# First batch of a windowed attention: values on 64 rows, probabilities copied unscattered, another order of steps

## The chip, the core and the metric

The kernel runs on one core of one Trainium2 chip. A core has a matrix engine (TensorE, PE in the profile; its weight loads are listed apart as PEld), a vector engine (VectorE, DVE), a scalar engine (ScalarE, ACT), a general engine (GpSimd, POOL) and a queue that issues DMA transfers (SyncE, SP). The engines run side by side, each in its own order, and wait for one another through semaphores. PE reads SBUF and writes PSUM, an accumulation memory of eight banks of 512 float32 columns on 128 partitions; DVE and ACT read PSUM, POOL does not in this kernel. The metric is the device time of one execution in microseconds (us), the lower the better.

## The reference

Attention with a causal window over 8 batches, 8 heads, 576 positions and 64 columns, then a feed-forward layer over the 4608 tokens:

```python
rel = pos[:, None] - pos[None, :]
mask_plain = (rel >= 0) & (rel < window)
mask_dil = (rel >= 0) & (rel < window * dilation) & (rel % dilation == 0)
masks = np.stack([mask_plain if h < H // 2 else mask_dil for h in range(H)], axis=0)
scores = np.where(masks[None, :, :, :], scores, -1000000000.0)
scores = scores - np.max(scores, axis=-1, keepdims=True)
attn = np.exp(scores)
attn = attn / (np.sum(attn, axis=-1, keepdims=True) + 1e-09)
return np.matmul(attn, v).astype(np.float32)
...
h = x @ w_in
g = np.where(h > 0.0, h, alpha * (np.exp(np.minimum(h, 0.0)) - 1.0))
return (g @ w_out).astype(np.float32)
```

The window is 32 positions, the dilation 4, so every query sees at most 32 keys. For the heads with dilation the kernel orders positions by residue, so that their window is one of 32 neighbours too. The weights are 512 x 2048 and 2048 x 512, and arrive as 64-bit words that the kernel turns into float32.

## The kernel before

**Tiling of the attention.** Heads are taken in pairs (`hp` 0 to 3), one head on rows 0 to 63 and one on rows 64 to 127. The 576 queries of a pair are 6 units (`NU`) of 96 (`QB`), each of 3 blocks (`GU`) of 32 (`G`). A block of 32 queries sees 64 keys: its own 32 and the 32 before.

**The first batch** is written out by hand in `first_attention` (line 338), a generator for each pair, and the main loop (line 951) names the steps in order. A letter and a pair's number is a step:
- S: scores, 36 small matmuls on top of a mask that two matmuls lay into PSUM (each float32 matmul has two records in the trace).
- M: DVE takes the maxima and subtracts them (lines 356, 359), ACT takes the exponential (361). Here a load of weights is issued too, held by a small POOL copy (119) behind the maxima.
- P: DVE sums (363), adds 1e-9 (326), takes reciprocals (327); the multiply (328) is DVE's for pairs 0 and 3 and POOL's for pairs 1 and 2.
- T: PE transposes the probabilities, 12 matmuls against an identity, and the first head's four copies follow; U: the second head's four. These copies (381 on DVE, 383 on ACT) scatter the 64 keys x 96 queries of a unit into a tile `pt` of 128 keys x 96 queries, where each block of 32 queries has its own 64 rows and the rest was set to zero.
- O: 12 matmuls of values (128 keys x 64) against those tiles, 96 columns each, and the copies to `x32`, the layer's input (314, 317).
- G: one term of the first product of the feed-forward layer (f = 0) for one pair; A, B, C, D: parts of the conversion of the first weights (A on ACT, line 136; B to D on DVE, lines 144, 152, 154).

All of these are marked so that each engine keeps them in program order. PSUM is shared by name: scores go to `a` or `b`, transposes to `c` or `a`, outputs to `d` or `b`, so an odd pair's transposes need `a` free and its outputs `b`.

**What follows.** The layer runs over chunks of 512 tokens; f counts the 16 slices of 128 hidden columns. Only pair 0 to 3 of the first batch feed the first chunk. Meanwhile DVE and ACT convert and split the weights (`magnitude`, `convert`, `split_w`) and do the second batch's attention (`second_attention`), whose order a planner sets from modelled times. The second batch's loads reuse the buffers `qt`, `kt` and `vt` of the first; weights go through rings `r0` to `r3`, of which `r2` and `r3` hold pairs 2 and 3 of the first batch until their outputs are made.

**Loads.** SP issues, in order, the masks, q and k of the four pairs, v of pairs 0 and 1, the first weights, v of pairs 2 and 3 (line 937).

Of the kernel before, what the change touches and what calls it, by code (L numbers as in the profile page):

```python
# [10 lines left out]
F32 = mybir.dt.float32  # L11
# [5 lines left out]
ALU = mybir.AluOpType  # L17

B, H, S, D = 8, 8, 576, 64
WINDOW, DIL = 32, 4  # L20
NCLS = S // DIL
DM, DFF = H * D, 2048
NT = B * S
P = 128
G = 32
QB = 3 * G
NU = S // QB
NPAIR = H // 2
NA = 3
GU = QB // G  # L30
# [30 lines left out]
WHEN = {1: (0, 6, 7, 13), 2: (0, 6, 7, 12)}  # L61
EARLY = 14
LAST = 14
OPER = 12
PLAIN = ("a5", "a-1'")
BLOCKS = [(b, hp) for b in range(CS + 1, B) for hp in (0, 2)]
# [5 lines left out]


@with_exitstack
def body(ctx: ExitStack, tc: tile.TileContext, q, k, v, masks, w_in, w_out, out):
    nc = tc.nc
    const = ctx.enter_context(tc.tile_pool(name="const", bufs=1))
    wst = ctx.enter_context(tc.tile_pool(name="wst", bufs=1))
    ap = ctx.enter_context(tc.tile_pool(name="ap", bufs=2))
    xp = ctx.enter_context(tc.tile_pool(name="xp", bufs=1))  # L80
# [8 lines left out]
    mask_sb = masks_sb[:, :2 * NU * 2 * G].rearrange("p (d m) -> p d m", d=2)  # L89
    ones_sb = masks_sb[:, 2 * NU * 2 * G:]  # L90
    ident = const.tile([QB, QB], F32, name="ident")

    pt = [const.tile([P, 2 * NU, QB], F32, name=f"pt{i}") for i in range(2)]

    early2 = [wst.tile([P, 2, 4 * DM], F32, name=f"r{NR - NE + i}") for i in range(NE)]
    early = [early2[i // 2][:, i % 2, :] for i in range(2 * NE)]
# [9 lines left out]
    def inorder(ins):  # L106
        tc.keep_in_program_order(ins)
        return ins
# [145 lines left out]
    last_transpose = [None] * B  # L254
    count = [0]

    def room(b, hp):
        i = b * NPAIR + hp
        if i in (2, 3):
            e = early[2 * (i - 2):]  # L260
            return e[0][:, :S], e[0][:, S:WINDOW + 2 * S], e[1][:, :2 * NU * D].rearrange("p (u d) -> p u d", u=2 * NU)
        return ap.tile([P, S], F32, name="qt"), ap.tile([P, WINDOW + S], F32, name="kt"), ap.tile([P, 2 * NU, D], F32, name="vt")


    qk_of, v_of = {}, {}
# [55 lines left out]
    def outputs(b, hp, places, vt, tr, keep=lambda ins: ins):  # L321
        products(places, vt, tr)
        return copies(b, hp, places, keep)

    def normalise(eng, sm, sums, keep):
        keep(nc.vector.tensor_scalar(out=sums, in0=sums, scalar1=1e-9, scalar2=None, op0=ALU.add))
        keep(nc.vector.reciprocal(out=sums, in_=sums))
        return keep(eng.tensor_tensor(out=sm, in0=sm, in1=sums.unsqueeze(2).broadcast_to([QB, 2 * NU, 2 * G]), op=ALU.mult))

    def transposed():  # L330
        count[0] += 1
        return pt[count[0] % len(pt)]
# [5 lines left out]
    def first_attention(hp, loaded):  # L338

        dil = hp >= NPAIR // 2  # L340
        qt, kt, vt = loaded
        if hp > 0:
            room, o = (early[0], WINDOW + 2 * S) if hp == 1 else (early[2 * (hp - 2) + 1], 2 * NU * D)
            sm = room[:QB, o:o + 2 * NU * 2 * G].rearrange("p (u j) -> p u j", u=2 * NU)
        else:
            sm = ap.tile([QB, 2 * NU, 2 * G], F32, name="sm", bufs=1)
        mx = ap.tile([QB, 2 * NU], F32, name="nmx", bufs=4)
        sums = ap.tile([QB, 2 * NU], F32, name="sums", bufs=4)
        s_ps = ps_f.tile([P, 2, TC], F32, name="ab"[hp % 2])[:QB, :, :NU * 2 * G]
        for h in range(2):  # L350
            mm(s_ps[:, h, :], ones_sb, mask_sb[:, int(dil), :], start=True, stop=False)
        scores([s_ps[:, h, :] for h in range(2)], qt, kt, False)
        yield
        s4 = s_ps.rearrange("p h (n j) -> p h n j", n=NU)
        mx4 = mx.rearrange("p (h n) -> p h n", h=2)
        inorder(nc.vector.tensor_reduce(out=mx4, in_=s4, op=ALU.max, axis=mybir.AxisListType.X))
        if hp > 0:
            load_w(hp, mx)
        inorder(nc.vector.tensor_tensor(out=sm.rearrange("p (h n) j -> p h n j", h=2), in0=s4,
                                        in1=mx4.unsqueeze(3).broadcast_to([QB, 2, NU, 2 * G]), op=ALU.subtract))  # L360
        inorder(nc.scalar.activation(out=sm, in_=sm, func=AF.Exp, scale=0.125))
        yield
        inorder(nc.vector.tensor_reduce(out=sums, in_=sm, op=ALU.add, axis=mybir.AxisListType.X))
        last = normalise(nc.vector if hp in (0, NPAIR - 1) else nc.gpsimd, sm, sums, inorder)
        if hp == NPAIR - 1:
            last_step[hp] = last.ins
        yield
        tr = transposed()

        t_ps = (ps_c, ps_f)[hp % 2].tile([P, 2, TC], F32, name="ca"[hp % 2])  # L370
        for n in range(NU):
            for h in range(2):
                o = n % NA * QB
                mm(t_ps[h * 2 * G:(h + 1) * 2 * G, n // NA, o:o + QB], sm[:, h * NU + n, :], ident, start=True, stop=True)
        t4 = t_ps[:, :, :NA * QB].rearrange("p i (n q) -> p i n q", n=NA)
        for h in range(2):
            to = tr[:, h * NU:(h + 1) * NU, :].rearrange("p (i n) q -> p i n q", i=2)
            for c, r, m in ((0, 0, 2), (1, 0, 1), (1, 1, 1), (2, 0, 2)):
                cs, ks, rs = slice(c * G, (c + 1) * G), slice((c + r) * G, (c + r + m) * G), slice((h * 2 + r) * G, (h * 2 + r + m) * G)
                if hp == NPAIR - 1 or (hp, h) == (1, 0):  # L380
                    inorder(nc.vector.tensor_copy(out=to[ks, :, :, cs], in_=t4[rs, :, :, cs]))
                else:
                    inorder(nc.scalar.copy(out=to[ks, :, :, cs], in_=t4[rs, :, :, cs]))  # L383
            yield
        a_ps = ps_f.tile([P, 2, TC], F32, name="db"[hp % 2])
        yield outputs(0, hp, [(a_ps[:, i, :], i * NA, (i + 1) * NA) for i in range(NU // NA)], vt, tr, inorder)

    def exponential(u, sm, nmx, sums):
        nc.scalar.activation(out=sm[:, u, :], in_=sm[:, u, :], func=AF.Exp, bias=nmx[:, u:u + 1], scale=0.125, accum_out=sums[:, u:u + 1])
# [542 lines left out]
                    load_v(i + 2)  # L932
            yield state[-1]

    rooms = [room(0, hp) for hp in range(NPAIR)]

    for what in "m0 qk0 qk1 qk2 qk3 v0 v1 w0 v2 v3".split():
        i = int(what[-1])
        if what[0] == "m":
            nc.sync.dma_start(out=masks_sb, in_=masks)  # L940
            nc.gpsimd.tensor_tensor(out=ident, in0=ones_sb, in1=ones_sb, op=ALU.mult)
        if what[0] == "w":
            load_w(i)
        for t, src in zip("qkv", (q, k, v)):
            if t in what:
                nc.sync.dma_start(out=rooms[i]["qkv".index(t)], in_=src[i])
    x32[0] = xp.tile([P, NPAIR, S], F32, name="x32", bufs=2)
    its = [first_attention(hp, rooms[hp]) for hp in range(NPAIR)]


    for what in "S0 S1 M0 M1 S2 P0 M2 T0 U0 S3 P1 P2 A0 M3 T1 U1 O0 T2 U2 P3 B0 O1 T3 U3 O2 G0 G1 O3 G2 A1 C0 D1".split():
        i = int(what[1])
        if what == "G0":
            ps_second.close()
            ps_h = ctx.enter_context(tc.tile_pool(name="ps_h", bufs=1, space=bass.MemoryType.PSUM, side="right"))
            first = product1(0, 0)
        if what[0] == "A":
            inorder(magnitude(i))
        elif what[0] in "BCD":
            last_conversion = convert(i // 2, inorder, {"B": slice(0, DM), "C": slice(DM, 2 * DM), "D": slice(2 * DM, 4 * DM)}[what[0]])  # L960
        elif what[0] == "G":
            next(first)
        else:
            last_copy = next(its[i])
# [117 lines left out]
def _layout(q, k, v):  # L1082


    order = np.arange(S).reshape(NCLS, DIL).T.reshape(-1)

    inner = np.arange(G).reshape(G // DIL, DIL).T.reshape(-1)
    plain = (np.arange(0, S, G)[:, None] + inner[None, :]).reshape(-1)
    qs = np.empty((B, NPAIR, 2 * D, S), np.float32)
    ks = np.zeros((B, NPAIR, 2 * D, WINDOW + S), np.float32)  # L1090
    vs = np.empty((B, NPAIR, P, 2, NU, D), np.float32)
    for hp in range(NPAIR):
        dil = hp >= NPAIR // 2
        hs = slice(2 * hp, 2 * hp + 2)
        qo, ko = (order, order) if dil else (plain, np.arange(S))
        qs[:, hp] = q[:, hs][:, :, qo].transpose(0, 1, 3, 2).reshape(B, 2 * D, S)
        ks[:, hp, :, WINDOW:] = k[:, hs][:, :, ko].transpose(0, 1, 3, 2).reshape(B, 2 * D, S)
        vv = np.zeros((B, 2, WINDOW + S, D), np.float32)
        vv[:, :, WINDOW:] = v[:, hs][:, :, ko]
        for n in range(NU):  # L1100
            vs[:, hp, :, :, n] = vv[:, :, n * QB:n * QB + P].transpose(0, 2, 1, 3)
    pairs = B * NPAIR
    return qs.reshape(pairs, P, S), ks.reshape(pairs, P, WINDOW + S), vs.reshape(pairs, P, 2 * NU, D), order


def _masks():
# [32 lines left out]
```

## Time and profile before

| | |
|---|---|
| median of 3 runs | 878.44 us (877.64 to 880.87) |
| profiled execution | 878.75 us |
| its span | 877.0 us |
| mean granted clock of PE | 0.995 |
| busy: PE, PEld, DVE, ACT, POOL | 97%, 82%, 63%, 62%, 4% of the span |
| chain that ended last, PE's part | 85% of the span |

The span runs from the first to the last instruction; a row of the profile names line, engine, operation, output and inputs, shapes, and how many instructions it holds, and a bracket at its end the idle time ahead of it and who ended that. Matmuls are pipelined, so that neighbouring rows of PE may overlap a little.

### The profile page before, as it was taken

The numbers are of one execution on the slowest core, as the hardware profiler recorded it, in microseconds if no ns is written. First come the engines' busy times: TensorE is split into PE (matmuls) and PEld (weight loads), VectorE is DVE, ScalarE is ACT, GpSimd is POOL, SyncE is SP. The second block draws the span as 40 slices with busy tenths as digits, with TensorE's granted clock in tenths as the row PEclk, the third lists the DMA queues.
The fourth block names the chain that finished last, engine by engine and source line by source line (L and its number), as shares of the span: only waits on it lengthen the run. The fifth ranks groups of instructions, "written<-read, shape, count | busy, mean of one in ns | idle before, by whom it ended". The sixth has DMA issues, their size and how long they took to land.

```text
span 877.0 us, 17535 instructions
## 1 busy us (share of the span) xinstructions
PE 854.6 (97%) x6788; PEld 721.9 (82%) x6788; DVE 553.5 (63%) x906; ACT 544.7 (62%) x1067; POOL 34.9 (4%) x72
## 2 busy tenths in 40 slices
PE   6999989999999999999999999999999999999998
PEld 4556777778878888898878899988898988999986
DVE  6899977657585866788665476645476645344431
ACT  3778977867576766666664565654466754555541
POOL 2000000000000000110010010100011100000000
PEclk8999999999999999999999999999999999999999
DMA  9997435032555256877753877762875652776541
GB/s 346 384 363 265 140 105 188 31 122 90 169 188 186 99 166 190 271 226 246 223 199 86 264 224 234 204 200 72 252 238 177 207 163 86 230 211 195 144 149 58
DMA packets 93459, 166.48 MB, mean 190 GB/s; under 512 B 9696, under 2 KB 40768, under 8 KB 93376
## 3 DMA queue, kind: packets, MB, share of 16 engines
q1 hardware_dynamic: 89200, 158.01, 56.8%
q10 hardware_dynamic: 4176, 7.34, 2.3%
q8 instruction: 54, 0.88, 0.4%
q14 instruction: 29, 0.24, 0.1%
HBM read 124.42 MB, written 40.89 MB: 189 GB/s over the span
## 4 chain that ended last, share of the span: by engine, by line
PE 85%; DVE 5%; ACT 5%; issue 2%; DMA 1%; SPq 0%; POOL 0%; ACTq 0%; DVEq 0%
PE o_ps L111 42%; PE h L111 35%; PE a_ps L111 8%; ACT pt L435 1%; DMA kt<-k 1%; DMA out<-e 1%; DVE nmx L410 1%; DVE sm L397 0%; ACT pt L383 0%; ACT h L624 0%; ACT gh L642 0%; DVE a L152 0%; ACT a L191 0%; ACT a L448 0%; ACT e L636 0%
## 5 line engine op out<-in xcount | busy, mean ns | idle before, releaser
L111 PE MATMUL h<-xall,r 128*128 128x384 f32 (+1 forms) x708 | 157.0, 363 | 1.2 <-ACT h L624 0.8
L111 PEld LDWEIGHTS h<-xall,r 128*128 128x128 f32 x708 | 127.4, 188 | 18.7 <-ACT h L624 1.2
L111 PE MATMUL o_ps<-a,gh 128*128 128x512 f32 x394 | 128.9, 416 | 0.0
L448 DVE SCALAR_TENSOR_TENSOR a-1_3369<-a-1_3369,a 128x768 f32<-128x768 f32 x64 | 61.0, 953 | 87.8 <-ACT a L448 87.8
L111 PE MATMUL h<-r,r 128*128 128x384 f32 x476 | 108.2, 336 | 1.0 <-DVE gl L448 0.9
L448 ACT COPY e<-h 128x384 f32<-128x384 f32 x96 | 46.0, 479 | 98.3 <-PE h L111 96.4
L448 ACT ACTIVATE a<-a-1_3369 128x384 f32<-128x384 f32 (+1 forms) x96 | 60.9, 634 | 50.1 <-DVE a-1_3369 L448 44.1
L111 PEld LDWEIGHTS o_ps<-a,gh 128*128 128x128 f32 x394 | 73.4, 188 | 21.8 <-issue 9.1
L111 PEld LDWEIGHTS h<-r,r 128*128 128x128 f32 x476 | 84.4, 188 | 4.3 <-DVE r L448 1.2
L111 PE MATMUL o_ps<-r,gh 128*128 128x512 f32 x242 | 75.3, 392 | 0.0
L111 PE MATMUL o_ps<-a,r 128*128 128x512 f32 x288 | 72.2, 392 | 0.0
L111 PE MATMUL o_ps<-a,gl 128*128 128x512 f32 x173 | 67.7, 391 | 0.0
L448 ACT ACTIVATE a<-a 128x768 f32<-128x768 f32 (+1 forms) x72 | 60.8, 845 | 1.9
L111 PEld LDWEIGHTS o_ps<-a,r 128*128 128x128 f32 x288 | 53.6, 188 | 9.9
L111 PE MATMUL h<-a,r 128*128 128x384 f32 x256 | 60.1, 335 | 0.0
L448 DVE TENSOR_TENSOR a-1_3369<-h,e 128x384 f32<-128x384 f32 x64 | 35.1, 549 | 35.5 <-PE h L111 35.5
L111 PEld LDWEIGHTS o_ps<-r,gh 128*128 128x128 f32 x242 | 44.9, 188 | 8.6
L111 PEld LDWEIGHTS h<-a,r 128*128 128x128 f32 x256 | 46.4, 188 | 4.2
L111 PE MATMUL o_ps<-r,gl 128*128 128x512 f32 x117 | 45.9, 392 | 0.2 <-DVE gl L448 0.2
L637 DVE SCALAR_TENSOR_TENSOR e<-h,e 128x512 f32<-128x512 f32 x30 | 20.6, 686 | 30.1 <-ACT e L636 29.9
L111 PE MATMUL o_ps<-a,xall 128*128 128x512 f32 x153 | 39.5, 393 | 0.0
L111 PEld LDWEIGHTS o_ps<-a,gl 128*128 128x128 f32 x173 | 32.5, 188 | 6.8
(217 smaller groups left out, 1531.3 us busy)
## 6 DMA issues: line engine op xcount, KB each, us to landing
r<-combined SPq DMA_DIRECT2D x224, 256.0 KB, 3.5
aside<-a-1_3369 SPq DMA_DIRECT2D x64, 192.0 KB, 3.3
vt<-v SPq DMA_DIRECT2D x30, 384.0 KB, 4.2
kt<-k SPq DMA_DIRECT2D x30, 304.0 KB, 4.7
qt<-q SPq DMA_DIRECT2D x30, 288.0 KB, 4.0
r<-w_in SPq DMA_DIRECT2D x16, 512.0 KB, 7.8
r<-w_out SPq DMA_DIRECT2D x16, 512.0 KB, 8.2
combined<-a SPq DMA_DIRECT2D x20, 256.0 KB, 3.0
```

The source lines that it names most:

```text
L111: return inorder(nc.tensor.matmul(*args, **kw))
L410: nc.vector.tensor_reduce(out=nmx, in_=sm, op=ALU.max, axis=mybir.AxisListType.X)
L435: last_transpose[b] = nc.scalar.copy(out=tr[ks, :, cs], in_=sm[cs, :, rs]).ins
L448: return lambda *args, **kw: inorder(getattr(self.eng, name)(*args, **kw))
L637: v.scalar_tensor_tensor(out=e, in0=h_ps, scalar=0.0, in1=e, op0=ALU.max, op1=ALU.subtract)
```

## The change

- **Values.** For the first batch the host lays out the values once more (`v0`): for each of 18 blocks of 32 queries its own 64 keys x 64 columns, one head of a pair on rows 0 to 63, the other on rows 64 to 127. A pair's load is 128 x 1152 float32 in place of 128 x 768. Pairs 0 and 1 keep it in one buffer of `x32` (which has two), pairs 2 and 3 where they had it.
- **Copies.** The transposed probabilities are copied as they stand in PSUM, two copies of 128 x 288 on ACT for a pair (step K), into a third of `turned`, a tile that takes the place of weights needed later. Nothing is scattered.
- **Outputs.** O becomes 36 matmuls for a pair, of 64 keys x 64 columns against 32 columns of `turned`; the copies to `x32` are a step of their own (X).
- **Normalising.** 1e-9 is added from a tile `least`; pair 0's multiply goes to POOL, so that only pair 3's stays on DVE.
- **Order.** The steps stand in another order (`SEQ`); S3 is ahead of the first transposes, and outputs, copies and transposes of different pairs alternate.

```diff
+SEQ = "S0 S1 M0 M1 S2 P0 M2 S3 T0 K0 P1 M3 O0 X0 T1 A0 K1 P2 O1 X1 P3 B0 T2 K2 T3 O2 K3 X2 G0 O3 A1 G1 G2 X3 C0 D1"
...
+    least = const.tile([QB, 2 * NU], F32, name="least")
+    nc.gpsimd.memset(least, 1e-9)
...
-    def room(b, hp):
-        i = b * NPAIR + hp
-        if i in (2, 3):
-            e = early[2 * (i - 2):]
-            return e[0][:, :S], e[0][:, S:WINDOW + 2 * S], e[1][:, :2 * NU * D].rearrange("p (u d) -> p u d", u=2 * NU)
-        return ap.tile([P, S], F32, name="qt"), ap.tile([P, WINDOW + S], F32, name="kt"), ap.tile([P, 2 * NU, D], F32, name="vt")
+    shared = xp.tile([P, 2, NU * GU * D], F32, name="x32", bufs=2)
+
+    def room(hp):
+        if hp > 1:
+            e = early[2 * (hp - 2):]
+            return e[0][:, :S], e[0][:, S:WINDOW + 2 * S], e[1][:, :NU * GU * D]
+        return ap.tile([P, S], F32, name="qt"), ap.tile([P, WINDOW + S], F32, name="kt"), shared[:, hp, :]
...
-    def normalise(eng, sm, sums, keep):
-        keep(nc.vector.tensor_scalar(out=sums, in0=sums, scalar1=1e-9, scalar2=None, op0=ALU.add))
+    def normalise(eng, sm, sums, keep, least=None):
+        if least is None:
+            keep(nc.vector.tensor_scalar(out=sums, in0=sums, scalar1=1e-9, scalar2=None, op0=ALU.add))
+        else:
+            keep(nc.vector.tensor_tensor(out=sums, in0=sums, in1=least, op=ALU.add))
...
-        last = normalise(nc.vector if hp in (0, NPAIR - 1) else nc.gpsimd, sm, sums, inorder)
+        last = normalise(nc.vector if hp == NPAIR - 1 else nc.gpsimd, sm, sums, inorder, least)
...
-        t4 = t_ps[:, :, :NA * QB].rearrange("p i (n q) -> p i n q", n=NA)
-        for h in range(2):
-            to = tr[:, h * NU:(h + 1) * NU, :].rearrange("p (i n) q -> p i n q", i=2)
-            for c, r, m in ((0, 0, 2), (1, 0, 1), (1, 1, 1), (2, 0, 2)):
-                cs, ks, rs = slice(c * G, (c + 1) * G), slice((c + r) * G, (c + r + m) * G), slice((h * 2 + r) * G, (h * 2 + r + m) * G)
-                if hp == NPAIR - 1 or (hp, h) == (1, 0):
-                    inorder(nc.vector.tensor_copy(out=to[ks, :, :, cs], in_=t4[rs, :, :, cs]))
-                else:
-                    inorder(nc.scalar.copy(out=to[ks, :, :, cs], in_=t4[rs, :, :, cs]))
-            yield
+        yield
+
+        tr = turned[:, hp % 3 * S:(hp % 3 + 1) * S]
+        for i in range(NU // NA):
+            inorder(nc.scalar.copy(out=tr[:, i * NA * QB:(i + 1) * NA * QB], in_=t_ps[:, i, :NA * QB]))
+        yield
         a_ps = ps_f.tile([P, 2, TC], F32, name="db"[hp % 2])
-        yield outputs(0, hp, [(a_ps[:, i, :], i * NA, (i + 1) * NA) for i in range(NU // NA)], vt, tr, inorder)
+        vt = vt.rearrange("p (n c d) -> p n c d", n=NU, c=GU)
+        for n in range(NU):
+            for c in range(GU):
+                for h in range(2):
+                    hs, o = slice(h * D, (h + 1) * D), n % NA * QB + c * G
+                    mm(a_ps[hs, n // NA, o:o + G], vt[hs, n, c, :], tr[hs, n * QB + c * G:n * QB + (c + 1) * G], start=True, stop=True)
+        yield
+        yield copies(0, hp, [(a_ps[:, i, :], i * NA, (i + 1) * NA) for i in range(NU // NA)], inorder)
...
-        for t, src in zip("qkv", (q, k, v)):
+        for t, src in zip("qkv", (q, k, v0)):
...
+    turned = wst.tile([P, 4, DM], F32, name="a5").rearrange("p t c -> p (t c)")
...
-    for what in "S0 S1 M0 M1 S2 P0 M2 T0 U0 S3 P1 P2 A0 M3 T1 U1 O0 T2 U2 P3 B0 O1 T3 U3 O2 G0 G1 O3 G2 A1 C0 D1".split():
+    for what in SEQ.split():
```

More of the change, by code (lines that the diff above doesn't have):

```diff
@@ L74, in body @@
 @with_exitstack
-def body(ctx: ExitStack, tc: tile.TileContext, q, k, v, masks, w_in, w_out, out):
+def body(ctx: ExitStack, tc: tile.TileContext, q, k, v, v0, masks, w_in, w_out, out):
     nc = tc.nc
@@ L342, in first_attention @@
         if hp > 0:
-            room, o = (early[0], WINDOW + 2 * S) if hp == 1 else (early[2 * (hp - 2) + 1], 2 * NU * D)
+            room, o = (early[0], WINDOW + 2 * S) if hp == 1 else (early[2 * (hp - 2) + 1], NU * GU * D)
             sm = room[:QB, o:o + 2 * NU * 2 * G].rearrange("p (u j) -> p u j", u=2 * NU)
@@ L367, in first_attention @@
         yield
-        tr = transposed()
         t_ps = (ps_c, ps_f)[hp % 2].tile([P, 2, TC], F32, name="ca"[hp % 2])
@@ L933, in second_attention @@
             yield state[-1]
-    rooms = [room(0, hp) for hp in range(NPAIR)]
+    rooms = [room(hp) for hp in range(NPAIR)]
     for what in "m0 qk0 qk1 qk2 qk3 v0 v1 w0 v2 v3".split():
@@ L1101, in _layout @@
             vs[:, hp, :, :, n] = vv[:, :, n * QB:n * QB + P].transpose(0, 2, 1, 3)
+    at = np.arange(NU)[:, None] * QB + np.arange(GU) * G + np.arange(2 * G)[:, None, None]
+    first = np.empty((NPAIR, 2, 2 * G, NU, GU, D), np.float32)
+    for hp in range(NPAIR):
+        vv = np.zeros((2, WINDOW + S, D), np.float32)
+        vv[:, WINDOW:] = v[0, 2 * hp:2 * hp + 2][:, order if hp >= NPAIR // 2 else np.arange(S)]
+        first[hp] = vv[:, at]
     pairs = B * NPAIR
-    return qs.reshape(pairs, P, S), ks.reshape(pairs, P, WINDOW + S), vs.reshape(pairs, P, 2 * NU, D), order
+    return qs.reshape(pairs, P, S), ks.reshape(pairs, P, WINDOW + S), vs.reshape(pairs, P, 2 * NU, D), first.reshape(NPAIR, P, NU * GU * D), order
 def _masks():
@@ L1124 @@
     from concourse.bass_utils import run_bass_kernel_spmd
-    qs, ks, vs, order = _layout(q, k, v)
+    qs, ks, vs, first, order = _layout(q, k, v)
     w_in = moe_w_in.reshape(NC, P, NF, P).transpose(2, 1, 0, 3).reshape(NF, P, DM)
-    arrays = {"q": qs, "k": ks, "v": vs, "masks": _masks(), "w_in": np.ascontiguousarray(w_in).view(np.int64),
+    arrays = {"q": qs, "k": ks, "v": vs, "v0": first, "masks": _masks(), "w_in": np.ascontiguousarray(w_in).view(np.int64),
               "w_out": np.ascontiguousarray(moe_w_out.reshape(NF, P, DM)).view(np.int64)}
```

## The prediction, made before the result was known

> **What bounds the kernel now.** I read the busy shares first, then busy times by stretch, TensorE's waits, and the engines' instructions in order of time. These are the busy shares; the busy times of two stretches (in order PE, PEld, DVE, ACT, POOL, clock, DMA share, GB/s); and the waits of PE.
>
> ```profile
> PE 854.6 (97%) x6788; PEld 721.9 (82%) x6788; DVE 553.5 (63%) x906; ACT 544.7 (62%) x1067; POOL 34.9 (4%) x72
> ...
> 0.00:28.20 28.20, 18.94 (x464) 15.14 (x464) 19.66 (x34) 13.20 (x30) 6.02 (x12) 0.88 0.95 358
> 28.20:48.00 19.80, 18.75 (x139) 9.18 (x138) 17.66 (x28) 12.81 (x21) 0.00 (x0) 1.00 1.01 382
> ...
> PE o_ps L111 <- DVE gl L643: 2.6, 1, 2.6
> ...
> PE h L111 <- DVE h L193: 1.0, 1, 1.0
> ...
> PE h L111 <- DVE e L634: 0.3, 1, 0.3
> ```
>
> PE is busy for 97% of the span, so a gain can only come from the little time in which it waits. 9.3 of that lie in the first 28.2 us (28.20 less 18.94), which is the stage that the change rewrites. Three later waits are for DVE: 1.0, 0.3 and 2.6, together 3.9 us, all ahead of products of the first chunk (L193 makes its weights, L634 and L643 its activations). The rows that set the order of the first stage, PE first:
>
> ```profile
> 10.17 1.52 PE L111 MATMUL a<-r 64*32 64x64 f32 x72
> 13.94 1.21 PE L111 MATMUL c<-ident,sm 96*64 96x96 f32 x24 [2.25 <-DVE sm L328]
> 15.08 0.87 PE L111 MATMUL b<-masks_sb 96*96 96x384 bf16 x2
> ...
> 18.61 2.19 PE L111 MATMUL a<-ident,r 96*64 96x96 f32 x24 [1.21 <-POOL r L328]
> 22.24 1.16 PE L111 MATMUL c<-ident,r 96*64 96x96 f32 x24
> ...
> 28.23 1.98 PE L111 MATMUL h<-x,a 128*128 128x512 f32 x4
> 30.15 1.21 PE L111 MATMUL b<-pt,r 128*64 128x96 f32 x24
> 31.29 5.43 PE L111 MATMUL h<-x,a 128*128 128x512 f32 x12
> 36.65 0.97 PE L111 MATMUL a_ps<-kt,qt 64*32 64x64 f32 x72
> ...
> 12.35 0.17 DVE L326 TENSOR_SCALAR sums<-sums 96x12 f32<-96x12 f32 x1
> 12.55 0.22 DVE L327 RECIPROCAL sums<-sums 96x12 f32<-96x12 f32 x1
> 12.81 0.95 DVE L328 TENSOR_TENSOR sm<-sm,sums 96x768 f32<-96x768 f32 x1
> 13.68 0.95 DVE L356 TENSOR_REDUCE nmx<-a 96x12 f32<-96x768 f32 x1
> 14.66 0.95 DVE L359 TENSOR_TENSOR r<-a,nmx 96x768 f32<-96x768 f32 x1
> 15.54 0.94 DVE L363 TENSOR_REDUCE sums<-r 96x12 f32<-96x768 f32 x1
> ...
> 17.78 0.80 DVE L326 TENSOR_SCALAR sums<-sums 96x12 f32<-96x12 f32 x1
> ...
> 20.92 1.44 DVE L381 COPY pt<-a 64x192 f32<-64x192 f32 x4 [0.28 <-PE a L111]
> ...
> 24.71 0.42 DVE L144 TENSOR_SCALAR a<-a 128x512 uint32<-128x512 uint32 x1
> ...
> 26.50 2.99 DVE L381 COPY pt<-a 64x192 f32<-64x192 f32 x8
> 33.18 0.69 DVE L144 TENSOR_SCALAR a<-a 128x1024 uint32<-128x1024 uint32 x1 [1.77 <-ACT a L136]
> ...
> 15.65 0.84 ACT L361 ACTIVATE r<-r 96x768 f32<-96x768 f32 x1 [3.33 <-DVE r L359]
> 16.40 2.64 ACT L383 COPY pt<-c 64x192 f32<-64x192 f32 x8
> 19.06 1.14 ACT L136 ACTIVATE a<-r 128x1024 f32<-128x1024 f32 x1
> 23.80 0.70 ACT L317 COPY x<-d 128x288 f32<-128x288 f32 x2
> ...
> 17.09 1.47 POOL L328 TENSOR_TENSOR r<-r,sums 96x768 f32<-96x768 f32 x1 [2.22 <-ACT pt L383]
> ```
>
> The last row of products, at 31.29, holds 12 records of the first gemm: four that end f = 0, eight that are f = 1. At 5.36/12 = 0.447 us each, f = 0 ends at 33.1: my mark for PE. My mark for DVE is 33.18, the conversion D1, which waits for ACT's A1, which stands behind the last copy of the attention. From D1 DVE works almost without a gap until PE's 1.0 us wait, so DVE sets the end as much as PE.
>
> **What the change does, step by step.** Scattering goes: eight copies a pair (2.64 on ACT; 1.44 and 2.99 on DVE) become two of 128x288, 0.70 a pair as in the row of L317. One multiply moves from DVE (0.95) to POOL (1.47). The sum with 1e-9 took 0.17, but 0.80 beside POOL's multiply; its tensor form I put at 0.17, bounds 0.17 and 0.80. DVE sheds 1.44 + 2.99 + 0.95 + 0.63 = 6.0 us, ACT 2.64 x 2 + 1.32 (half as many copies for pair 1) less 4 x 0.70 = 3.8.
>
> The products change from 24 records of 96 columns (1.20 us) to 72 of 32 columns, weights of 64 columns on 64 rows. No row shows them. The scores, also 72 records on 64 rows, took 0.97, 13.5 ns each, with weights of half as many columns; a record of the transposes, weights of 64 columns over 96 rows, took 1.16/24 = 48 ns. So the bounds are 0.97 and 72 x 48 = 3.5. I take 1.8, 25 ns a record: the score's record doubled for twice the columns, which is also the transposes' record halved for two halves of rows.
>
> [...]
>
> Now the new order, from the first place where it differs. S3 follows S2 (11.7), so it is done by 14.1. On DVE an M takes 1.86 (13.68 to 15.54), a P without its multiply 1.4 (0.94 + 0.17 + 0.22 and gaps), a conversion like B0 1.8 (24.71 to 26.50). So it runs M2 at 12.8 (no multiply before it), P1 at 14.7, M3 at 16.1, P2 at 18.0, P3 at 19.3 to 21.7 with its multiply, B0 and C0 until 25.3. POOL gives the first multiply at 14.3, P1's at 17.6, P2's at 20.9.
> PE and ACT: T0 14.35 to 15.5, K0 to 16.25, O0 to 18.1 and T1 to 19.3. On ACT the exponential of M3 stands ahead of X0 (18.0 to 18.85), then X0 to 19.55, A0 to 20.65, K1 to 21.35: PE idles two us and O1 runs 21.35 to 23.15. This added wait holds T2 behind O1 although its data is there at 20.9.
>
> The clock belongs in this sum. Granted clock by stretches (busy PE, clock, DMA share, GB/s):
>
> ```profile
> 11.60:15.00 3.40, 1.15 (x30) 1.00 1.01 403
> 15.00:18.40 3.40, 2.40 (x78) 0.52 1.05 393
> 18.40:21.90 3.50, 3.29 (x42) 0.50 1.03 408
> ```
>
> After a stretch with 1.15 us of work the clock was half for two stretches, and T1 took 2.19; T2 at 22.24, at full clock again, 1.16. In the new order 11.6 to 15 is full of S3 and T0, but 18.4 to 21.9 holds only 0.9 of T1 and 0.55 of O1. I let the clock fall at 21.9 for one stretch: T2 takes 2.2, to 25.35. Bounds: nothing, or T3 and O2 slow too (2.0 more). Then K2 to 26.1, T3 to 26.55, O2 to 28.35, X2 to 29.1, G0 to 29.3, O3 to 31.1, G1 and G2 to 32.9, the fourth term to 33.8 (X3 is done by 31.85). f = 0 ends **0.7 later** than the mark. A1 runs 29.1 to 30.25, so D1 starts at 30.3, **2.9 earlier**: DVE, not PE, gains.
>
> DMA: the values grow by half.
>
> ```profile
> vt<-v SPq DMA_DIRECT2D x1, 384.0 KB, 6.9
> ...
> 4.98 1.49 SPq L946 DMA_DIRECT2D vt<-v  x2
> 14.50 0.33 SPq L122 DMA_DIRECT2D r<-w_in  x1
> 15.74 0.33 SPq L122 DMA_DIRECT2D r<-w_out  x1
> ...
> r<-w_in SPq DMA_DIRECT2D x1, 512.0 KB, 8.7
> ...
> r<-w_out SPq DMA_DIRECT2D x1, 512.0 KB, 8.8
> ```
>
> Two weight loads land at 23.2 and 24.5, so 512 KB pass in 1.3 us with the queues full (DMA share about 1). Four times 192 KB more are 1.9 us. The second batch's first two value loads no longer wait for a buffer, so SP may issue their 768 KB ahead of these weights: 1.9 more. A1's weights then land at 26.4 to 28.4, before 29.1: hidden by the attention. Values of pair 0 land at 11.9 + 0.5, O0 begins at 16.3: hidden. If the cover goes, D1 is late by what lands after 29.1.
>
> Sum: +0.7 for PE's path; -1.0, since DVE is 2.9 ahead when PE waits for L193; of the two later waits (2.9), DVE's remaining lead, 2.9 - 0.3 = 2.6, can take 2.6; I take 2.1, since part can be lost to instructions that wait for PE itself (bounds 0 and 2.6). Together **-2.4**: span 877.0 to 874.6. The profiled execution took 878.75, 1.75 more than its span, and lies 0.3 over the median of 878.44; from the median the forecast is **876.0 us**.
>
> **Rivals.** (1) *Products one after another*, 3.5 us each: the end lies on the slower side. O0 ends at 19.8, K1 at 22.4, O1 at 25.9, O2 at 31.8, O3 at 36.2, f = 0 at about 39.0, 5.9 late; all of the 3.9 us of waits vanish, so +2.0: 880.4, and 884.3 if they stay. It decides from about 2.9 us a product, where 3.9 are lost. For it: both heads write one PSUM bank in one stretch, where the scores keep a bank for each. Against: their rows and output partitions are disjoint.
> [...]
> (2) *Transfers take the lead*: weights for the next conversions land 1.9 to 3.9 later and DVE waits for ACT, which waits for them; DVE's lead is gone, and PE's 0.7 is lost and at most the 1.0 won: 878.1 to 879.1, middle 878.6. For it: DMA share 1.01 until 48. This is also the case that the shorter copies bring nothing.
> (3) *Everything cheap*: products at 0.97 and full clock. ACT's chain still holds O1 to 21.35; O2 ends at 25.7, f = 0 at 31.2, 1.9 early; D1 starts 3.5 early; with the waits PE could win 5.8, DVE 3.5 to 6.0 (what it sheds). Taken 4.9: 873.5.
>
> **Chances.** Forecast 0.46; (1) 0.14; (2) 0.15; (3) 0.25. The range 872.4 to 881.0 leaves out about 0.05 of (1) and 0.1 of (3). A measurement here tells 0.5%, 4.4 us, from no change: faster 0.25 (0.2 of (3), 0.05 of the forecast's tail), slower 0.06 (from (1) and a clock that stays low), within 0.69.
>
> **What would show it.** Products of 72 records at 1.8 us (0.97: rival 3; 3.5: rival 1). K of 0.7 a pair. PE idle about 2 us ahead of O1, and a clock of 0.5 after it. D1 near 30.3 and f = 0 ending near 33.8. The wait for L193 gone, the 2.6 us wait for L643 mostly gone. I am wrong if DVE waits for L136 with late loads, or if a scheduler's other order of later instructions moves more than these 4 us.

## The result: 1.3% slower

| | before | after |
|---|---|---|
| median, us | 879.65 (877.64 to 881.47) | 891.24 (890.27 to 891.48) |
| span of the profiled execution, us | 877.0 | 889.7 |
| mean granted clock of PE | 0.995 | 0.983 |
| f = 0 of the layer's first product ends at, us | 33.1 | 47.8 |

The ratio is 1.013 [1.0103, 1.0157], from four runs of each. All four runs of the changed kernel have a mean granted clock of 0.981 to 0.986. The busy shares of the changed kernel:

```profile
PE 868.3 (98%) x6980; PEld 735.2 (83%) x6980; DVE 548.4 (62%) x893; ACT 541.0 (61%) x1055; POOL 36.8 (4%) x74
```

Its two first stretches (start and end, length, then busy PE, PEld, DVE, ACT, POOL, clock, DMA share, GB/s):

```profile
0.00:28.20 28.20, 18.45 (x466) 15.35 (x468) 17.10 (x27) 7.67 (x12) 7.48 (x14) 0.78 0.96 369
28.20:48.00 19.80, 19.80 (x228) 15.38 (x226) 3.33 (x4) 6.77 (x14) 0.00 (x0) 0.54 0.65 238
```

Two of PE's waits (in total, times, longest):

```profile
PE b L115 <- DVE nmx L364: 3.5, 1, 3.5
...
PE o_ps L115 <- DVE gl L653: 2.8, 2, 1.5
```

DVE and ACT shed 5.1 and 3.7 us, about what was forecast (6.0 and 3.8), but PE is busy 13.7 us longer. The second stretch tells where: PE works all 19.80 us at a mean clock of 0.54, and DVE, which did 17.66 us of work there before, does 3.33. Busy PE is here slow PE. The same first stage instruction by instruction (start, duration, engine, line, product, records, wait ahead):

```profile
14.07 0.53 PE L115 MATMUL b<-masks_sb 96*96 96x384 bf16 x2 [3.46 <-DVE nmx L364]
...
15.42 2.06 PE L115 MATMUL c<-ident,sm 96*64 96x96 f32 x24
17.97 1.81 PE L115 MATMUL d<-a,x 64*64 64x32 f32 x29 [0.49 <-ACT a L386]
20.37 2.55 PE L115 MATMUL d<-a,x 64*64 64x32 f32 x43 [0.59 <-issue]
22.85 2.19 PE L115 MATMUL a<-ident,r 96*64 96x96 f32 x24
25.54 4.05 PE L115 MATMUL b<-a,x 64*64 64x32 f32 x72 [0.50 <-ACT a L386]
29.52 2.19 PE L115 MATMUL c<-ident,r 96*64 96x96 f32 x24
31.49 2.13 PE L115 MATMUL a<-ident,r 96*64 96x96 f32 x24
33.55 4.05 PE L115 MATMUL d<-a,r 64*64 64x32 f32 x72
37.54 2.07 PE L115 MATMUL h<-x,a 128*128 128x512 f32 x2
39.54 4.05 PE L115 MATMUL b<-a,r 64*64 64x32 f32 x72
43.52 7.65 PE L115 MATMUL h<-x,a 128*128 128x512 f32 x14
...
39.41 0.69 DVE L148 TENSOR_SCALAR a<-a 128x1024 uint32<-128x1024 uint32 x1 [11.02 <-ACT a L140]
...
47.78 0.60 ACT L637 ACTIVATE e<-h 128x512 f32<-128x512 f32 x1 [1.41 <-PE h L115]
```

A step O takes 4.05 us, where 1.8 was forecast; every T takes over 2 us. f = 0 ends when ACT can take its output, at 47.78, 14.7 us behind before's mark. D1, forecast for 30.3, begins at 39.41, because A1 stands behind the copies of O2 on ACT. The granted clock by stretches (length, PE busy, clock, DMA share, GB/s):

```profile
11.60:15.00 3.40, 0.93 (x48) 1.00 1.02 413
...
18.40:21.90 3.50, 2.91 (x56) 0.50 1.03 404
...
28.70:32.10 3.40, 3.40 (x50) 0.50 0.80 312
32.10:35.50 3.40, 3.40 (x57) 0.50 0.06 20
...
42.30:45.70 3.40, 3.40 (x29) 0.50 1.03 386
45.70:49.10 3.40, 3.40 (x8) 0.91 0.95 330
```

The records of the clock put the fall at 15.6 us and the return at 46.3: 30.7 us at half, where before had 6.8 (15.1 to 21.9). From 25.54 on, 20 us, the rows above show no idle time of PE. The DMA share of 0.06 at 32 to 35 us is a consequence: SyncE waits 8.9 us, until the end of O2 at 37.7, to issue the next weights into a buffer that O2 reads.

How much of this reaches the end? I follow the issue of each store to `out`, after less before, in us:

```
store           0      4      8     12     18     24     36
before at   145.9  246.0  346.5  443.4  579.8  713.4  874.1
after       +12.0  +12.3  +12.2  +10.4  +11.4  +12.8  +12.8
```

Of the 14.7 lost by 47.8, 2.7 are won back by the first store (1.1 of them from the waits for DVE that the prediction named, 3.9 in before and 2.8 now; the rest I didn't trace; ACT felt only 12.7 of the 14.7, since in before it took f = 0's output no earlier than 35.12). From then on the difference stays between 10.4 and 12.8. So the loss is made in the first stage.

### The profile page after: what moved, and what is told of

The parts are those of the page before. It is cut to its first block, busy times and chain, and to the rows that moved or that the text cites. A ratio compares the mean times of both kernels' runs of the same rounds, so it can differ in the third digit from the quotient of the medians.

```text
span 889.7 us, 17891 instructions
## 1 busy us (share of the span) xinstructions
PE 868.3 (98%) x6980; PEld 735.2 (83%) x6980; DVE 548.4 (62%) x893; ACT 541.0 (61%) x1055; POOL 36.8 (4%) x74
## 4 chain that ended last, share of the span: by engine, by line
PE 83%; DVE 5%; DMA 5%; ACT 4%; issue 2%; SPq 1%; ACTq 0%; DVEq 0%
PE o_ps L115 39%; PE h L115 33%; PE a_ps L115 8%; PE b L115 1%; DMA r<-combined 1%; PE d L115 1%; DMA kt<-k 1%; DMA r<-w_out 1%; DMA whole<-a 1%; DVE a L158 1%; DVE a L156 1%; ACT pt L445 1%; DMA out<-e 1%; PE a L115 1%; DMA qt<-q 0%
## 5 line engine op out<-in xcount | busy, mean ns | idle before, releaser
L115 PEld LDWEIGHTS h<-xall,r 128*128 128x128 f32 x708 | 127.5, 188 | 18.7 <-issue 1.6
L458 ACT ACTIVATE a<-a-1_3443 128x384 f32<-128x384 f32 (+1 forms) x96 | 60.9, 634 | 51.2 <-DVE a-1_3443 L458 45.1
L445 ACT COPY pt<-sm 32x384 f32<-32x384 f32 x72 | 36.7, 510 | 3.2 <-DVE sm L442 2.4
```

The costliest lines, as they stand in the source:

```text
L115: return inorder(nc.tensor.matmul(*args, **kw))
L445: last_transpose[b] = nc.scalar.copy(out=tr[ks, :, cs], in_=sm[cs, :, rs]).ins
L458: return lambda *args, **kw: inorder(getattr(self.eng, name)(*args, **kw))
```

## The experiments

All times are beside the kernel before, run on the same chip (its medians were 879.6 to 879.9). A product step is one O, 72 records. Each experiment's trace is of one execution.

### The price of the products by itself: e1_prices

Blocks of matmuls on constants are put into the second chunk of the kernel before: `small` has the form of the new products, `turning` that of the transposes, `wide` that of the old products, `scored` that of the scores.

```diff
+    def small(to, n):
+        for i in range(18 * n):
+            for h in range(2):
+                hs, o = slice(h * D, (h + 1) * D), i % 9 * G
+                mm(to[hs, o:o + G], probe[hs, :D], probe[hs, D:D + G], start=True, stop=True)
...
+            if (c, f) == (1, 3):
+                small(banks()[0], 10)
+                turning(banks()[0], 12)
+                wide(banks()[0], 14)
+            if (c, f) == (1, 10):
+                scored(banks(), 14)
```

> The kernel before, with blocks of extra matmuls of constants in the second chunk, where PE runs at full clock: ten times the 72 records of the new products, twelve times the 24 of the transposes, fourteen times the 24 of the old products, and later fourteen times the 72 of the scores. Theory A (the clock): the new products take about 2.0 us at full clock, 28 ns a record, and 4.05 only once the clock has fallen; although PE is never idle in their block, the granted clock falls to 0.5 in it within 7 us, and it comes back in the block of old products. Theory B (the form): they take 4.05 us from the first on, one record after another, and the clock stays at 1.0 through all blocks.

It took 977.34 us, in one run. Windows of PE alone (length, busy, clock, DMA share, GB/s): one ahead of the fall of the clock, two in the small products, one in the other two forms.

```profile
159.00:160.20 1.20, 1.12 (x39) 1.00 0.00 0
162.00:178.00 16.00, 16.00 (x305) 0.50 0.06 18
182.00:196.00 14.00, 14.00 (x268) 0.50 0.01 2
202.00:224.00 22.00, 21.93 (x532) 1.00 0.01 3
```

At full clock 39 records took 1.12 us, 29 ns each, so 2.1 us a step; at half 16.00/305 = 52 ns, 3.8 us a step. That is Theory A's price. The block began at full clock behind a wait of 2.4 us, the clock fell 1.2 us into it, and it stayed at half for 41.0 us (160.3 to 201.2). PE was busy nearly all that time (16.00 of 16.00 and 14.00 of 14.00 us in the two windows), with next to no transfers beside it (share 0.06 and 0.01). Full speed was back sooner than expected, not with the old products but 4.4 us after the transposes' form began at 196.8. What made the clock fall there isn't shown, since the wait stands just ahead of it. But that it stayed down is no matter of contention or of waiting: **once the clock was down, the new products didn't bring it back**, in the 36.5 us from 160.3 to 196.8.

### The new products in the old order: e3_old_order

```diff
-SEQ = "S0 S1 M0 M1 S2 P0 M2 S3 T0 K0 P1 M3 O0 X0 T1 A0 K1 P2 O1 X1 P3 B0 T2 K2 T3 O2 K3 X2 G0 O3 A1 G1 G2 X3 C0 D1"
+SEQ = "S0 S1 M0 M1 S2 P0 M2 T0 K0 S3 P1 P2 A0 M3 T1 K1 O0 X0 T2 K2 P3 B0 O1 X1 T3 K3 O2 X2 G0 G1 O3 X3 G2 A1 C0 D1"
```

> The changed kernel with its steps in the order of before (S3 behind the first transposes, K in the place of the old copies, X behind O). Theory A (the small products never bring the clock back): the clock is 0.5 from about 15 us until the first gemm, products take about 4 us, 886 to 893 us. Theory C (the new order idles PE and so lowers the clock): the clock is back by 25 us, 874 to 880 us.

896.17 us (893.38 to 900.09), ratio 1.0193 [1.0158, 1.0229]. The products in order of time:

```profile
20.77 2.29 PE L115 MATMUL d<-a,x 64*64 64x32 f32 x72
...
24.12 1.23 PE L115 MATMUL b<-a,x 64*64 64x32 f32 x35
25.91 1.24 PE L115 MATMUL b<-a,x 64*64 64x32 f32 x37 [0.56 <-issue]
...
28.23 2.17 PE L115 MATMUL d<-a,r 64*64 64x32 f32 x66
31.79 0.36 PE L115 MATMUL d<-a,r 64*64 64x32 f32 x6 [1.40 <-issue]
...
33.99 2.29 PE L115 MATMUL b<-a,r 64*64 64x32 f32 x72
```

Here the clock was back at 20.1 and held, and a step takes 2.29 us: that is its price at full clock, 32 ns a record. f = 0 ends at about 38.0, 4.9 late, mostly by the four products: 9.6 us here, 6.1 in before. Two waits lie in the middle of a step, at instructions 962 and 1218 of PE (its weight loads and its waiting instructions counted too), 256 apart; more on them below. Both theories missed: the clock did as Theory C said, but the time lies above both ranges. The difference grows from 7.4 at the first store to 14.7 at the end; that growth is new, and e8 takes it up. The trace is of the fastest of four runs (893.38; the others took 894.28 to 900.09 at mean clocks of 0.981 to 0.994), so that the clock held is seen in that one alone.

### The old products in the new order: e4_old_products

The loads, copies, values and products of before, under the changed kernel's `SEQ` and normalising:

```diff
-        tr = turned[:, hp % 3 * S:(hp % 3 + 1) * S]
+        tr = transposed()
...
+        products([(a_ps[:, i, :], i * NA, (i + 1) * NA) for i in range(NU // NA)], vt, tr)
```

> The changed kernel in its new order and with POOL's multiply of pair 0, but with the old values, scattered copies and products of 96 columns. Theory A: the clock may fall near 15 us and is back within two stretches of 3.4 us once products of 128 rows run; 875 to 881 us. Theory C (the order is at fault): the clock stays low until the gemm, 886 to 892 us.

891.33 us (890.27 to 891.75), ratio 1.0133 [1.0115, 1.015]. The time is Theory C's, but the run doesn't separate what it should. The order was made for short copies, and with the scattering ones PE waits for ACT (3.1 and 0.8 us for `pt`), the T's and the old products run at half clock (2.19 us and more; 2.02 for 21 records of O0) until 34.0, and f = 0 ends at 41.0. So with waits between them the old products, too, stayed at half clock: the form of the new ones is not the only thing that can go with a low clock. And of the 12.7 us by which it ends late, 4.1 come behind the first store. It shows only that the order isn't good by itself.

### Work to hold the clock: e5_burst

```diff
+    def burst(n):
+        z = rooms[3][1]
+        to = ps_c.tile([P, 2, TC], F32, name="c")
+        for k in range(n):
+            mm(to[:, k % 2, :448], z[:, 32:32 + P], z[:, 160:608], start=True, stop=True)
...
+        if what == "T0":
+            burst(5)
```

> The changed kernel with five extra matmuls of 128 rows x 128 x 448 columns between S3 and the first transposes, into a bank that nobody has used yet. Theory A (half a clock is most of the loss): they bring the clock back by 23 us, at a cost of about 6 us; from there a product takes 2.3 us in place of 4.05, and f = 0 ends near 40 us instead of 47.8; 880 to 887 us in all. If the clock is only a symptom, f = 0 ends at 53 us or later and the time is 895 or more.

895.84 us (894.77 to 897.95), ratio 1.017 [1.0144, 1.0196].

```profile
24.46 2.29 PE L115 MATMUL d<-a,x 64*64 64x32 f32 x72 [0.49 <-ACT a L386]
...
28.86 2.83 PE L115 MATMUL b<-a,x 64*64 64x32 f32 x72 [0.97 <-ACT a L386]
...
35.66 4.05 PE L115 MATMUL d<-a,r 64*64 64x32 f32 x72
```

The burst did bring the clock back, at 20.3, and O0 took the 2.29 of e3. It fell again at 30.6, in O1, after a wait of 0.97, and stayed low to 51.0. So the price of 2.29 holds in the new order too, and the clock was lost again between small products and short waits. The burst cost 5.70 us of its own, so nothing is gained: f = 0's output is taken at 51.2, later than the 40 of Theory A, and the time is that of the other expectation, the clock as a symptom. It doesn't prove that one, since the clock was low again for 20.5 us.

### Is the wait ahead of S3 one for DVE? e6_early

The profile puts PE's 3.46 us ahead of S3 down to DVE. But the last reader of bank `b` was done long before that:

```profile
10.28 0.95 DVE L367 TENSOR_TENSOR r<-b,nmx 96x768 f32<-96x768 f32 x1
```

It ended at 11.23; S3 began at 14.07. S3's first instruction is number 450 of PE; the wait of 0.59 in O0 stands at number 706, 256 further on, and e3's two at 962 and 1218. 48 tiny matmuls (96 instructions) ahead of S0 move all numbers:

```diff
+    to = ps_c.tile([P, 2, TC], F32, name="c")
+    for t in range(48):
+        mm(to[:QB, t % 2, :G], ones_sb, ones_sb[:, :G], start=True, stop=True)
```

> The changed kernel with 48 tiny bfloat16 matmuls (96 instructions) ahead of S0, where PE waits for q and k. Theory D (PE's code comes in blocks of 256 instructions, and the waits at PE's instructions 450 and 706 are for code): the long wait leaves S3's start and stands at PE's instruction 450, now in the middle of S2, about 1 us shorter or more; the next at 706. If S3 waits for DVE instead, its wait of 3.5 us stays at S3. Time 884 to 893 us, by whether the clock falls.

903.25 us (896.44 to 904.62), ratio 1.0231 [1.0179, 1.0283].

```profile
14.12 0.74 PE L115 MATMUL a<-r 64*32 64x64 f32 x48 [1.45 <-issue]
14.78 0.53 PE L115 MATMUL b<-masks_sb 96*96 96x384 bf16 x2
...
20.16 1.87 PE L115 MATMUL c<-ident,sm 96*64 96x96 f32 x19 [3.10 <-issue]
```

S3 (the row at 14.78) now has no wait, though DVE is the same; the waits moved into the middle of S2 and of T0, to instructions 450 and 706, as Theory D said. **PE waited for its program.** (The time is above the 884 to 893 expected: f = 0 is taken at 51.3, and behind the first store the difference grows from 18.7 to 24.6, which is e3's matter again.) When the block starts:

```
PE instruction       450     706     962    1218
before             13.83   20.75   30.36   47.83
after              14.07   20.36   28.66   37.00
e3_old_order       14.88   20.88   25.91   31.79
e6_early           14.12   20.16   29.78   38.12
```

Instruction 450 comes at 13.8 to 14.9 whatever it is, and 706 6.0 to 6.9 us later; 47.83 in before is a wait for DVE. The traces hold the loads of the program as well, packets of 16384 bytes (`q8 instruction` in the view of the DMA queues). Ahead of each of these waits one landed 1.3 to 1.5 us before the block began: at 12.64 and 19.08 in after, at 12.64 and 18.79 in e6, at 24.64 and 30.32 ahead of e3's 25.91 and 31.79. In before number 450 is the first instruction of T0, which waited for probabilities until 13.76 anyway, so that its row couldn't tell; the change puts S3 there, whose data was ready.

### Few products, the rest as changed: e7_few_products

```diff
-            for c in range(GU):
-                for h in range(2):
-                    hs, o = slice(h * D, (h + 1) * D), n % NA * QB + c * G
-                    mm(a_ps[hs, n // NA, o:o + G], vt[hs, n, c, :], tr[hs, n * QB + c * G:n * QB + (c + 1) * G], start=True, stop=True)
+            for h in range(2):
+                hs, o = slice(h * D, (h + 1) * D), n % NA * QB
+                mm(a_ps[hs, n // NA, o:o + QB], vt[hs, n, 0, :], tr[hs, n * QB:(n + 1) * QB], start=True, stop=True)
```

> The changed kernel, but each unit and head has one product of 64 rows and 96 columns against the first block's keys in place of three of 32 columns (keys of the other two blocks are left out): 24 records a pair as before, everything else as changed. If the number of products is the cost (72 records, 144 instructions), f = 0 ends by 37 us and the time is 875 to 881 us. If the half clock alone is, products of 64 rows do not bring it back either: the clock stays 0.5 until the gemm, f = 0 ends near 40 us and the time is 882 to 887 us.

880.56 us (878.14 to 882.15), ratio 1.0003 [0.9986, 1.0019].

```profile
14.05 0.53 PE L115 MATMUL b<-masks_sb 96*96 96x384 bf16 x2 [2.17 <-DVE nmx L364]
...
18.10 2.19 PE L115 MATMUL d<-a,x 64*64 64x96 f32 x24 [0.50 <-ACT a L386]
20.22 2.13 PE L115 MATMUL a<-ident,r 96*64 96x96 f32 x24
22.85 1.21 PE L115 MATMUL b<-a,x 64*64 64x96 f32 x24 [0.50 <-ACT a L386]
23.98 1.21 PE L115 MATMUL c<-ident,r 96*64 96x96 f32 x24
25.02 1.16 PE L115 MATMUL a<-ident,r 96*64 96x96 f32 x24
...
28.31 1.21 PE L115 MATMUL b<-a,r 64*64 64x96 f32 x24
29.45 6.28 PE L115 MATMUL h<-x,a 128*128 128x512 f32 x14
```

S3 is as late as in the changed kernel (14.05) and the clock falls at the same place (15.3), but it is back at 22.2. f = 0 ends at 29.45 + 6 x 0.447 = 32.1, 1.0 ahead of before and 15.7 ahead of after. So the fall of the clock isn't what the change brought; that it doesn't come back is. The time, too, is the one expected if the number of products is the cost. (The kernel leaves out the keys of two of three blocks, so it is no solution.) The two kernels differ in their edit only in the products, and the 15.7 us of the first stage can be laid out by rows. Products at full clock: 9.6 in e3 (2.29 + 2.47 + 2.53 + 2.29) against 4 x 1.21, **4.7**. The wait for code in O0: **0.6**. What half clock adds: products 16.5 less 9.6, less the 1.0 that e7's first one also lost, 5.9; transposes 8.6 against 6.7, 1.9; the eight records of f = 0 6.3 against 3.7, 2.6; together **10.4**.

The kernel as a whole gains nothing, though: 1.0 ahead at f = 0, 2.1 ahead at the first store, 2.5 behind at the end.

### What is lost later: e8_same_later and e9_few_one_more

The order of DVE's and ACT's later work isn't written out; it follows from modelled times. Compared instruction by instruction in the traces (store issues counted too), ACT's order is the same in before and after for the last 872 of 1035, but in e3, e4, e6 and e7 it is another, which agrees with that one only for the last 663, and in all four PE waits for ACT's copies of stores (4.9, 4.9, 4.8 and 1.8 us), which before and after don't. One product of 448 columns ahead of T0, in e5's form, moves the model's times: with it e3's ACT order agrees with after's for the last 1013. With it e7's agrees only for the last 617, so e9 has a third order, not the one that its expectation took it for.

```diff
 # e8: e3 with
+        if what == "T0":
+            burst(1)
 # e9: e7 with the same
```

> The changed kernel with the steps in the order of before (as in e3) and one product of 128x128x448 float32 ahead of T0, into a PSUM place that nothing reads. T0 waited 3.7 us for the probabilities there in e3, so the product lies in idle time on the chip (two records, 0.8 us at full clock, 1.6 at half). What it does is move the times by which the later work was laid out: with it the instructions of ACT and DVE behind the first stage stand in the order of before and after, where those of e3 stood in another. Theory F (the first stage loses 5 us at full clock, and what e3 lost behind it, 7.4 at the first store to 14.7 at the end, belongs to that other order of the later work): f = 0 ends 4 to 6 us later than before's mark of 33.1, the first store is 3 to 5 us later, the difference stays within 1.5 us of that to the end, and the waits of PE for the stores' copies (4.9 in e3) are gone: 882 to 885 beside 879.6. Rival G (what the first stage does in this order goes on to cost later, whatever the order behind it): the difference grows to 12 to 15 us again, 892 to 895. Rival H (the end of after is late by the order of its later work, not by its first stage): the end is more than 10 us late, though f = 0 is not.

> e7 (12 products of 64x64x96 a pair, the keys of blocks 1 and 2 left out) with one product of 128x128x448 float32 ahead of T0, into a PSUM place that nothing reads: 0.8 us at full clock, 1.6 at half, on PE's path here. The later order of ACT and DVE is then nearly that of before and after (DVE differs in the instructions 220 to 243 of 895, ACT in 272 to 299 of 1038, where e7 differed up to ACT's 374). Theory F (e7's lead of 2 us at the first stores was given back through the other order of its later work): first store 0.5 to 2 us earlier than before, and the end within 1.5 us of that difference: 877 to 879.5 beside 879.6. Rival G (a first stage of this kind gives its lead back whatever stands behind it): the end is 2 to 4 us later than before, 881 to 884.

e8: 888.12 us (886.5 to 888.97), ratio 1.0086 [1.0069, 1.0103]; e9: 880.61 us (878.77 to 884.23), ratio 1.0018 [1.0003, 1.0032]. The stores again, against before:

```
store               0      4      7      8     12     24     36
e3_old_order     +7.4   +9.9  +12.8  +14.1  +12.5  +14.7  +14.7
e4_old_products  +8.6   +9.8  +12.7  +12.8  +11.6  +12.7  +12.7
e6_early        +18.7  +21.5  +24.4  +24.7  +24.2  +24.6  +24.6
e8_same_later    +9.4   +9.4   +9.3   +9.3   +7.8  +10.3  +10.3
e7_few_products  -2.1   -1.6   +1.3   +1.2   +1.5   +2.5   +2.5
e9_few_one_more  +1.1   +2.0   +2.0   +2.6   +1.6   +1.8   +1.8
```

In e8 the difference hardly grows, and the waits for store copies are gone: e3's growth belonged to its other order of later work, not to its first stage. The four kernels with that order lose 2.8 to 4.2 between stores 4 and 8, whatever their first stage is; e8 and e9 lose 0.6 at most. The size in the expectation was missed, because the clock came late in e8 (22.9) and fell again at 29.7 for 10.2 us:

```profile
27.89 1.35 PE L115 MATMUL b<-a,x 64*64 64x32 f32 x38 [0.67 <-issue]
29.17 1.74 PE L115 MATMUL a<-ident,r 96*64 96x96 f32 x24
30.83 4.05 PE L115 MATMUL d<-a,r 64*64 64x32 f32 x72
34.81 3.78 PE L115 MATMUL h<-x,a 128*128 128x512 f32 x4
38.52 2.91 PE L115 MATMUL b<-a,r 64*64 64x32 f32 x72
41.37 5.43 PE L115 MATMUL h<-x,a 128*128 128x512 f32 x12
```

Its f = 0 ends at 41.37 + 4 x 0.45 = 43.2, 10.1 late, and the kernel's end is 10.3 late. Of the 5.2 beyond e3, 1.1 come from T0 beginning behind the added product (15.96, not 14.88); nearly all the rest are rows that e3 ran at full clock and e8 at half: the four records ahead of O3 1.8, T1 0.6, T3 0.5, O3 0.6.

e9 missed its first number and its time: f = 0 ends about 0.9 ahead, but the first store is 1.1 late. PE waited there once for a cause that the profile doesn't name (1.37 at 61.4), twice for `gl` (1.48 and 1.38) and once for ACT (1.02), more in all than before's 4.3. The first of these isn't for the program: no block begins there, and it ended as DVE and ACT were done with `a_ps` and `h` (61.26 and 61.29). A lead of one us on PE at 32 us wasn't kept in either of these two orders; in that of before and after it wasn't tried. No version that beats both kernels came out of this.

## Why the prediction was wrong

- **"I take 1.8, 25 ns a record"**: mis-sized. It measures 2.29 at full clock, 32 ns (e3, e5), inside the bounds of 0.97 and 3.5, and accounts for 4 x 0.5 = 2.0 us beyond the forecast.
- **"S3 follows S2 (11.7)"**: wrong by 2.4. PE's own program wasn't there, a term that the prediction didn't have. The trace of before could have told: instruction 450 begins there at 13.83, and the packet ahead of it landed at 12.54.
- **"I let the clock fall at 21.9 for one stretch"** is the step that failed most. It fell at 15.6 for nine stretches. The forecast took 11.6 to 15.0 as filled by S3 and T0; it held 0.93 us of work. And I let any busy stretch restore the clock, as the row 18.40:21.90 of before seemed to show; with products of 64 x 64 x 32 busy stretches didn't (e1: 16.00 of 16.00 us busy, at 0.50). The bounds, nothing or 2.0 more, left this out; by rows it is 10.4 of the 15.7 us that lie between after and e7 at f = 0.
- **K, the sum with 1e-9, POOL's multiply**: right. The copies take 0.70 a pair, the sum 0.17, or 0.53 where it stands beside POOL; the multiply 1.47.
- **"D1 starts at 30.3, 2.9 earlier"**: it follows O2 through X2 and A1, and so came 9 us late with it. DVE's lead never arose, and the terms of -1.0 and -2.1 went with it, though 1.1 us of those waits went for another reason: whoever is late waits less.
- **DMA**: hidden, as forecast. The loads of A1's weights landed at 26.4 and 27.6, within the span given; SP did issue the second batch's values ahead of them.
- **Rivals.** The first came nearest in time, with 3.5 a product and 5.9 late at f = 0, and the line on chances puts "a clock that stays low" beside it, without a price or a reason. Its mechanism wasn't it: a step at full clock takes 2.29, not 3.5, in one bank. Whether the bank accounts for a part of those 2.29 was not tried. The second and third fell. The last sign of being wrong, another order of later instructions, isn't what happened to this change (872 of ACT's 1035 agree), though it is worth 4 to 7 us in e3.

What stays open: why e3 kept its clock through waits of 0.56 and 1.40 between small products, where e5 and e8 lost it with 0.97 and 0.67; and why 4.0 us of transposes in a row (29.5 to 33.6 in after) didn't bring it back, where in e1 it was back 4.4 us after their start. One thing in the traces bears on both. The complete stretches of one clock were multiples of 3.41 us long: 3.41 and 6.83 in the first stage of before, 6.83 and 30.72 in that of after, 10.2 in e8 and 41.0 in e1 (3 and 12 times 3.41). Where they lie differs: the first record of full clock begins at 11.7 in before, at 8.8 in after, at 22.9 in e8. In e1 3.41 us of transposes alone (197.8 to 201.2) stood ahead of the return; in after, counted in lengths of 3.41 from 15.6, none held transposes alone (29.3 to 32.7 begins with the end of O1). Whether that is what kept the clock down isn't shown: no run moved these lengths against the work.

## What to carry to other kernels

Price small matmuls at both clocks (a step O: 2.29 and 4.05 us), and count a stage of them as one that may not win full clock back once it is lost (30.7 us at half in after, 41.0 in e1). Fewer and wider ones can be better, even if they compute more: before's 24 records of 96 columns took 1.2 us where the 72 of 32 take 2.3. Larger work put among the small did bring the clock back in e5, but cost 5.70 us, and the clock was lost again. Where a step is moved to fill a wait, look whether the wait sits at the same instruction number in the trace: then it can be the program that is late, and whatever is moved there waits too; the packets of the program in the trace tell (here they landed 1.3 to 1.5 us before the block began). When variants differ at the end but not at the stage that was changed, compare the order of the later instructions before a reason is looked for in the stage.

## What the hardware showed that I had not expected

- Half clock in spite of a busy engine: 41.0 us in e1 and the last 20 us to 46.3 in after.
- The supply of instructions. Where PE waited for them in the first 32 us, its blocks of 256 began 5.0 to 6.0 us apart (14.12 and 20.16 in e6; 20.88, 25.91 and 31.79 in e3), with a DMA share of 0.95 in e3 (0.94 from 28.2 to 48). With a share of 0.02 PE waited for them too: in e1's scores form the blocks (PE instructions 7362, 7618, 7874, 8130) began at 283.40, 286.86, 290.31 and 293.76, 3.45 us apart, each after 1.2 us without a start, so that PE was busy 14.09 of 20.00 us there, at half clock. Each block's packet landed 1.9 to 2.1 us after the block before had begun, and 1.3 to 1.6 us before its own first instruction.
- Data that was there 2.8 us earlier can stand in a row as what ended a wait (S3's 3.46 us, put down to DVE); in e6, where they fell in the middle of a step, the waits for the program stand as `issue`.
